# The last 64 tokens of two heads as one pair of 64-column tiles, x in nine blocks, and a new order

## The chip, the cores and the metric

The kernel runs on one core of a Trainium2 chip. The metric is the device time of the whole program in microseconds; lower is better. The core has five engines with queues of their own: TensorE (PE in the profile; its weight loads are PEld), VectorE (DVE), ScalarE (ACT), GpSimd (POOL) and SyncE (SP), which only issues transfers. Engines wait for one another through semaphores.

## The reference, cut to what matters

```python
def _attn_ref(q, k, v, w_phi):              # q, k, v: 8 x 8 heads x 576 tokens x 64; w_phi: 64 x 128
    def phi(x):
        proj = einsum('bhsd,df->bhsf', x, w_phi)
        proj = proj - max(abs(proj), axis=-1, keepdims=True)
        return concatenate([exp(proj), exp(-proj)], axis=-1)
    q_p, k_p = phi(q), phi(k)
    kv = einsum('bhsf,bhsd->bhfd', k_p, v)
    z = sum(k_p, axis=2)
    num = einsum('bhsf,bhfd->bhsd', q_p, kv)
    den = einsum('bhsf,bhf->bhs', q_p, z)[..., None] + 1e-06
    return num / den

# x: the heads of a token side by side, 4608 x 512; w1, w2, w3: 512 x 768; w_out: 768 x 512
h = maximum(maximum(x @ w1, x @ w2), x @ w3)
out = h @ w_out
```

## The kernel before

**Units and pairs.** The attention is cut into 16 units of four heads. The four heads are two pairs (`pr`), and in a pair two heads (`ab`) lie on the two halves of the partitions. A head has 576 tokens: 512 "main" tokens and a tail of 64. In the feature matrices `Eq` (one for each sign, `g`) the main tokens of a head fill four tiles of 128 columns, and the two tails of a pair lie side by side in one tile.

**One unit.** Loads of q, k and v; G, the projections of q and k for row sums of maxima and for `Ek` (`psq`, `psk`, L520: two matmuls side by side, each on 64 of the 128 rows of TensorE's array, form 64\*128); the maxima on VectorE (L539) and `Ek` on ScalarE (L533); the maxima of q carried into a row of `qkT` by a small DMA (`qkT<-mT`); M, the projection of q again (`psm`, L599) and `Eq` (L612); K, the accumulation of keys and values (`kvps`, L628, again pairs of 64\*128 matmuls, 72 to a unit); N, the numerators and the denominator of one head (`psn`, L646); x, a reciprocal and a product on VectorE (L652, L653); and X, which turns `x_sb` into `xT` by a transposing DMA (L676), for the first two units by TensorE (L666). The first four units turn q and k on TensorE (T, `tps`, L482), with matmuls on 64 of the 128 columns of the array (form 128\*64).

**N before.** There are four N in a unit, one for each head, with ten matmuls each: five tiles of 128 tokens times two signs. The fifth tile is the tail. Its left operand is 128 columns wide and begins at the tail of the head, so that half of its rows are of no use. x divides all five tiles, and a unit's `x_sb` has ten blocks of 128.

**The feed-forward part.** Chunk b takes 512 main tokens of both units of batch b, and a ninth chunk takes all tails, gathered by GpSimd into `x_last` (L816). A chunk is 12 groups of four matmuls (`ups`, L699) against w2-w1 and w3-w1, the maximum on VectorE and ScalarE into `hT`, and four or more groups of "straight" (`ops`, L726, x times the product of w1 and w_out) and "down" (`ops`, L731) with an eviction (L739) and a store (L746). The product of w1 and w_out stands in `xT` of the last batch until chunk 5 has read it, and is copied by GpSimd to `w_bf[0]` for the later chunks (L804).

**The order.** Nothing is scheduled at run time. `PLAN` is a table of words such as `1076G@2.9`: node number, engine letter (T is TensorE), numbers of the buffers that it takes, planned start. The program is written out in the order of the table, which gives each engine's order. `fill` puts matmuls without use (`idler`, L828) in TensorE's planned gaps early in the program.

Of the kernel before, what the change touches and what calls it, by code (L numbers as in the profile page):

```python
# [17 lines left out]
DM = H * D  # L18
DFF = 768
P = 128  # L20
# [19 lines left out]
EW = UT * P + D  # L40
XW = SM + P
# [55 lines left out]
0G@0.7 4A@0.7 6S0@0.7 10S0@1.1 2D7@1.1 86G1@1.2 3D@1.5 8S@1.5 13S@2.0 85G@2.0 361S1@2.4 15S0@2.8 1076G@2.9 159G0@3.6 7D2@3.7  # L97
5D@4.2 1G@4.5 158G@5.0 12D@5.1 1079G@5.8 16T5@5.8 17D2@6.5 27T015110@7.3 22T04@7.5 29A@7.8 30D@7.8 28A@8.3 14D@8.6 9A@8.8
26D@9.1 20T5@9.6 31D@9.7 18T6@9.7 24A@9.8 21D@10.3 228G2@10.5 19D@10.5 42T12@10.6 44A@11.0 32T56@11.3 11G@11.3 46D@11.4
1077G@11.4 33A@11.7 35D@11.7 43A@12.2 45D@12.3 23A@12.5 87D3@12.7 25D@12.8 37T31@12.8 88S@12.9 47A1@12.9 93T5@13.0 38A@13.3  # L100
40D@13.4 39A@13.9 94D0@13.9 58T41@14.1 50A0@14.3 41D@14.4 34A@14.5 89T3@14.6 59A@15.0 36D@15.1 55T2@15.2 90D@15.7 61T0@15.8
51A@15.8 60A@16.0 91T3@16.4 63A@16.5 48G@16.9 49D@16.9 67T4@16.9 56A@17.0 64T1@17.3 62A@17.5 68A@17.9 364G1@18.0 115T110601@18.1
69A@18.3 119D@18.5 54A@18.6 66A@18.7 118D@18.8 92D@19.1 53G@19.1 1086T0@19.3 65A@19.3 95T35@19.9 1087A1@20.0 105T71@20.1
52G@20.3 108D@20.6 116A@20.9 109D@21.2 117A@21.3 100T70@21.3 227G@21.4 102A@21.8 103D@21.8 1078G@22.2 57A@22.3 98D@22.4
110T76@22.5 97A@22.8 113D@23.0 162T2@23.1 106A@23.2 101A@23.7 137T30@23.8 163D2@23.8 96A@24.2 166T7@24.2 114D@24.4 164T4@24.5
139A@24.7 1090T2@25.0 167D@25.0 124A1@25.2 165D@25.3 138A@25.4 1088T7@25.5 126G1@25.6 1091A@25.9 70T043@26.0 1089D@26.2
125G@26.7 111A@26.8 140T2@27.2 107A@27.3 104D@27.4 1096T7@27.8 127G@27.8 141A@27.8 72D@28.0 142A@28.2 99D@28.3 112A@28.4
71D@28.9 173T003010@29.1 1097A@29.3 183T56@29.4 73T10@29.6 176D@29.7 174A@29.8 75T4@30.0 187D@30.2 120A@30.3 1094T3@30.4
175A@30.5 121G@30.7 186D@30.8 184A@31.0 160D0@31.4 177D@31.5 185A@31.6 161S@31.7 134T7@31.7 122G@31.8 74D1@32.1 362S1@32.1
79T5@32.2 135A@32.4 128T2@32.5 426S0@32.6 76D0@32.8 1095A@32.9 131T1@33.0 129A@33.4 77T0@33.5 297S0@33.5 80D0@33.5 178T43@33.8  # L110
136A@33.9 1082G@34.0 1098T6@34.1 229D1@34.2 181D@34.3 133A@34.4 182D@34.9 132A@34.9 123A@35.4 168T74@35.5 78D0@35.5 130A@35.6
143T015@35.8 170A@36.1 1080G@36.1 1099D@36.2 180A@36.5 172D@36.8 188T60@36.9 144A@37.2 192D@37.4 145A@37.4 231T2@37.6 191D@37.7
190A@37.8 1092T1@38.1 196A1@38.1 169A@38.3 232D0@38.3 198G0@38.4 189A@38.8 171D@38.9 148T51@39.5 1093A@39.7 152T4@39.8
149D1@40.0 83T0@40.1 199A@40.2 179A@40.4 146T6@40.4 197G@40.5 153D0@40.6 235T2@40.7 84A@40.8 150T1@40.9 236D@41.3 81T5@41.4
147D0@41.5 233T3@41.7 82A@41.9 151D1@42.1 193T6@42.3 154T2@42.4 365G@42.6 194A1@42.7 234D@42.7 242T104701@42.7 155A@43.0
237T10@43.1 195S@43.1 156T6@43.3 245D@43.3 238A@43.6 215T135@43.7 1081G@43.7 296S1@43.8 157D@43.9 243A@44.1 366S1@44.2 241D@44.4
252T24@44.9 246D@45.0 1104T6@45.1 217A@45.1 216A@45.4 255D@45.6 239A@45.7 1112T3@46.1 253A@46.2 240D@46.2 1105A0@46.6 1083D@46.8
247T10@46.9 254A@47.1 257T62@47.3 1110T5@47.4 250D@47.5 1085G@47.8 260D@48.1 203T11@48.4 251D@48.4 1102T6@48.6 1111A@48.6
230S@48.7 256D@49.0 249A@49.1 557S1@49.1 1116T5@49.4 1103A@49.7 1084D@49.9 363S2@50.1 244A@50.2 1114T6@50.3 1117D@50.6 248A@50.7
429G2@50.8 204A@51.1 261D@51.2 209T7@51.2 1124T4@51.4 1113D@51.5 259A@51.6 265A1@51.9 299G0@52.0 258A@52.1 1115D@52.1 262T0@52.3  # L120
1122T5@52.3 205A@52.4 263D0@52.7 210A@52.8 1125D@52.9 264S@53.1 300G@53.1 212T1@53.2 1108T6@53.3 211A@53.4 1123D@53.5 214A@53.9
200T2@54.2 213A@54.3 266G0@54.3 427S0@54.3 367T013010@54.4 1109D@54.4 201A@54.6 387T57@54.7 621S0@54.8 382T14@54.8 371D@55.0
1120T6@55.2 202A@55.2 556S1@55.2 391D@55.6 384A@55.7 385D@55.9 1106T2@56.0 388A@56.2 267G@56.4 383A@56.4 390D@56.5 1121D@56.9
1118T1@56.9 389A@56.9 369A@57.2 370D@57.5 1107A@57.6 377T56@57.8 206T7@58.1 386D@58.1 368A@58.1 1130T2@58.4 208A@58.6 301S2@58.6
380D@58.7 430G@59.1 379A@59.1 224T31@59.3 1119D@59.3 218T0@59.6 207A@59.6 281T50@59.9 225D1@59.9 269T4@60.0 268G@60.2 1131T@60.2
282A@60.2 1101G@60.5 271A@60.5 219D0@60.5 283A@61.0 381D@61.1 270A@61.2 372T57@61.5 624G1@61.7 1132A0@61.8 284T010@61.8
375D@62.1 298S0@62.3 374A@62.4 278T3@62.9 373A@62.9 286D@63.2 220T2@63.2 378A@63.4 376D@63.5 392T4@63.5 1126T0@63.7 279A@63.9
393D1@64.1 221D0@64.3 395A1@64.4 394S@64.5 272T7@64.5 285A@64.6 275T5@64.7 222T4@65.0 273A@65.0 428S3@65.2 287T60@65.3 276A@65.5
223D0@65.5 560G0@65.6 1127T@65.6 431S0@65.6 280A@65.9 288D0@66.3 274A@66.4 559G@66.7 307T104301@66.9 277A@66.9 302T17@67.2
1128A1@67.4 289T2@67.4 310D@67.5 396G0@67.8 291T5@67.8 304A@68.0 305D@68.0 1134T4@68.2 308A@68.5 292D1@68.6 303A@68.9  # L130
408T61@69.1 311D@69.3 1135T@69.3 226S@69.5 410A@69.5 290D0@69.9 397G@69.9 309A@70.0 409A@70.5 306D@70.5 293T5@70.6 322T13@70.9
1136A2@71.0 317T06@71.1 294D1@71.2 312T27@71.4 324A@71.6 1138T4@71.7 315D@71.8 318A@71.8 295S@71.9 398A@72.3 320D@72.4 313A@72.5
402T5@72.6 1139T@72.8 323A@72.9 325D@73.0 319A@73.2 492S0@73.3 316D@73.4 404A@73.7 491S0@73.7 326D@74.0 411T0@74.1 314A@74.2
414T021@74.2 1140D3@74.4 403A@74.6 321D@75.0 413A@75.1 405T5@75.4 412A@75.5 415D@75.7 416A@75.7 399T4@75.7 442T017010@76.0
330A0@76.0 561S1@76.2 400A@76.2 447T61@76.3 333G1@76.4 1152T3@76.5 446D@76.5 332G@76.7 401A@76.8 445D@77.1 449A@77.3 1150T2@77.5
1153D0@77.7 444A@77.8 407A@78.3 432T47@78.3 450D@78.3 1144T3@78.7 1151A@78.7 331G@78.8 435D@78.9 448A@79.2 436D@79.5 327T6@79.6
1148T4@79.7 443A@79.7 1129S@79.9 328D0@80.1 406A@80.2 451D@80.3 1162T2@80.5 1145A@80.7 329S@81.1 1149A@81.1 452T10@81.4
349T163@81.6 434A@81.6 1163D@81.7 493S2@81.8 433A@82.2 688S1@82.2 455D@82.3 456D@82.6 622S1@82.7 437T54@82.7 350A@83.0
494G0@83.2 582T101201@83.2 441D@83.2 453A@83.2 1146T7@83.3 454A@83.6 585D@83.8 1137S@83.9 438A@83.9 440D@84.1 421T60@84.3
495G@84.3 460A0@84.4 1164T1@84.6 439A@84.6 422D0@84.8 1147A@85.1 1141S@85.1 461G1@85.4 337T00@85.4 586D@85.4 351A@85.6  # L140
417T5@85.6 1165D@85.8 584A@85.9 457T6@86.0 334T7@86.0 339A@86.1 1156T4@86.2 418D0@86.4 336A@86.6 458D1@87.0 583A@87.1 340T1@87.1
419T5@87.3 1157D@87.3 335A@87.4 459S@87.4 423T6@87.6 338A@87.8 1158T3@87.9 420D0@88.0 1133S@88.1 342A@88.3 424D1@88.6 346T4@88.8
341A@88.9 343T0@88.9 1160T2@89.1 1159D@89.2 345A@89.4 496S2@89.4 625G@89.7 347A@89.9 1142T7@90.0 344A@90.1 1161D@90.2 348A@90.6
462G@90.8 567T56@90.8 1143D@91.1 572T31@91.2 577T04@91.4 569A@91.4 1154T2@91.6 575D@91.7 574A@91.9 570D@92.3 578A@92.4
# [137 lines left out]
def kernel(  # L282
# [94 lines left out]
    xT = const.tile([P, B, CT, XW], BF16, name="xT")  # L377


    line_w = [xT[:, B - 1, :, 0:DM], w_bf[0][:, :, 0:DM]]  # L380
    x_last = [w_bf[0][:, :, DM:DFF], const.tile([P, CT, DFF - DM], BF16, name="x_last")]

    def zeros():
# [476 lines left out]
```

## Time and profile before

| what | us |
|---|---|
| median of three runs | 288.84 (288.76 to 289.62) |
| the profiled execution, first to last instruction | 287.6 |
| PE busy | 275.5 (96%) |
| DVE, ACT, POOL busy | 205.7, 198.6, 117.1 |
| first matmul of chunk 0, of chunk 7 | 45.5, 245.9 |

The profiled execution is read by its own span of 287.6 us. The median of the runs is 1.24 us above it; launch and end, which have no instruction of the program, are taken to be that difference. A busy time of PE counts a matmul from its start to a modelled end, and matmuls overlap, so the distance from one start to the next is the better measure of what a matmul costs.

### The profile page before, as it was taken

To read this page: it belongs to the slowest core of one execution; us is meant where nothing else is said; L and a number is where in the kernel's file an instruction comes from. 1 tells how busy PE (TensorE), PEld (TensorE's weight loads), DVE (VectorE), ACT (ScalarE), POOL (GpSimd) and SP (SyncE) were. 2 spreads that over 40 slices of the span, in tenths; PEclk is the share of its full clock that TensorE was granted. 3 is DMA by queue.
4 is the path that set the end of the run, shared out by engine and by line. 5 is a ranking of instruction groups with operands and counts; after the bars stand their busy time and mean duration, and the time that the engine had idled before them with its cause. 6 is when DMAs were issued, how large, how long until landed. Compare 5 with 4: busy or idle time off the path is not lost.

```text
span 287.6 us, 8596 instructions
## 1 busy us (share of the span) xinstructions
PE 275.5 (96%) x3550; PEld 154.7 (54%) x3590; DVE 205.7 (71%) x434; ACT 198.6 (69%) x460; POOL 117.1 (41%) x100
## 2 busy tenths in 40 slices
PE   8889999999989899999999999999999999999995
PEld 3366675466555455655555466565544654444443
DVE  4679899988979788887879778987863551516511
ACT  1599998999998789895798979997756631040010
POOL 8264688868454349706365434050083000000000
PEclk9999999999999999999999999999999999999999
DMA  7999977999999998999899769787510019410054
GB/s 181 277 248 209 228 298 121 330 282 235 237 176 336 210 260 182 265 267 253 198 238 211 207 122 203 235 171 132 119 41 0 2 41 199 115 34 0 0 153 141
DMA packets 68337, 51.45 MB, mean 179 GB/s; under 512 B 48778, under 2 KB 53066, under 8 KB 68298
## 3 DMA queue, kind: packets, MB, share of 16 engines
q1 hardware_dynamic: 63903, 45.62, 65.6%
q0 software_dynamic: 4000, 4.92, 9.9%
q8 instruction: 28, 0.46, 0.7%
q10 hardware_dynamic: 395, 0.37, 0.4%
q14 instruction: 11, 0.09, 0.1%
HBM read 34.64 MB, written 9.44 MB: 153 GB/s over the span
## 4 chain that ended last, share of the span: by engine, by line
PE 87%; DMA 5%; DVE 3%; ACT 2%; issue 1%; SPq 0%; ACTq 0%; DVEq 0%
PE ups L699 31%; PE ops L731 16%; PE ops L726 10%; PE psn L646 7%; PE kvps L628 6%; PE psq L520 6%; PE psm L599 5%; DMA k_raw<-in_k_dram 3%; DMA qkT<-mT 2%; PE pm L797 2%; DVE mk L539 1%; PE tps L482 1%; DVE mqp L539 1%; ACT Ek L533 1%; ACT Eq L612 1%
## 5 line engine op out<-in xcount | busy, mean ns | idle before, releaser
L699 PE MATMUL ups<-xT,w_bf 128*128 128x512 bf16 x417 | 100.6, 379 | 0.8
L533 ACT ACTIVATE Ek<-psk 128x512 bf16<-128x512 f32 (+1 forms) x160 | 82.0, 572 | 15.3 <-PE psk L520 11.9
L574 POOL TENSOR_TENSOR vab<-v_raw,em 128x1152 bf16<-128x1152 f32 (+1 forms) x35 | 66.8, 1926 | 56.0 <-ACT em L570 45.9
L612 ACT ACTIVATE Eq<-psm 128x512 bf16<-128x512 f32 (+1 forms) x160 | 80.1, 577 | 10.4 <-PE psm L599 9.8
L699 PEld LDWEIGHTS <-w_bf 128*128 128x128 bf16 x432 | 40.2, 98 | 44.4
L539 DVE TENSOR_REDUCE mqp<-psq 128x4 bf16<-128x512 f32 (+1 forms) x80 | 48.5, 633 | 6.4 <-PE psk L520 4.7
L539 DVE TENSOR_REDUCE mk<-psk 128x4 f32<-128x512 f32 (+1 forms) x80 | 49.1, 630 | 5.0 <-PE psk L520 3.3
L731 PE MATMUL ops<-wout_bf,hT 128*128 128x512 bf16 (+2 forms) x219 | 49.8, 367 | 0.6 <-issue 0.3
L705 DVE TENSOR_TENSOR hT<-hT,ups 128x512 bf16<-128x512 bf16 x54 | 35.5, 681 | 16.8 <-PE ups L699 16.3
L739 ACT COPY osb<-ops 128x512 f32<-128x512 f32 (+2 forms) x18 | 10.0, 563 | 36.5 <-PE ops L731 28.9
L707 ACT ACTIVATE hT<-ups 128x512 bf16<-128x512 f32 x38 | 22.4, 612 | 15.5 <-PE ups L699 14.0
L731 PEld LDWEIGHTS <-hT 128*128 128x128 bf16 x228 | 21.1, 98 | 22.2
L653 DVE TENSOR_TENSOR x_sb<-psn,rden 128x320 bf16<-128x320 f32 x64 | 31.5, 492 | 2.2
L646 PEld LDWEIGHTS <-Eq 128*128 128x128 bf16 x640 | 25.9, 98 | 9.7
L739 DVE COPY osb<-ops 128x512 f32<-128x512 f32 (+1 forms) x20 | 13.4, 668 | 21.8 <-PE ops L731 21.6
L646 PE MATMUL psn<-kv_sb,Eq 128*128 128x65 bf16 x640 | 28.2, 194 | 0.0
L520 PE MATMUL psq<-w,qkT 64*128 64x128 bf16 x288 | 24.6, 217 | 2.2 <-DVE mk L539 0.8
L520 PEld LDWEIGHTS <-qkT 64*128 64x128 bf16 x576 | 16.8, 94 | 15.9 <-issue 11.9
L520 PE MATMUL psk<-w,qkT 64*128 64x128 bf16 x288 | 24.5, 217 | 0.2 <-DVE v_raw L460 0.2
L726 PE MATMUL ops<-xT 128*128 128x512 bf16 x85 | 23.1, 379 | 0.9 <-issue 0.5
L599 PE MATMUL psm<-qkT,wphi_m 128*128 128x512 bf16 (+1 forms) x70 | 22.1, 358 | 1.3 <-DMA qkT<-mT 1.2
L652 DVE RECIPROCAL rden<-psn 128x5 f32<-128x5 f32 x64 | 12.1, 189 | 11.8 <-PE psn L646 11.2
(74 smaller groups left out, 237.2 us busy)
## 6 DMA issues: line engine op xcount, KB each, us to landing
v_raw<-in_v_dram SPq DMA_DIRECT2D x16, 576.0 KB
out_dram<-osb SPq DMA_DIRECT2D x65, 128.0 KB
q_raw<-in_q_dram SPq DMA_DIRECT2D x12, 576.0 KB
k_raw<-in_k_dram SPq DMA_DIRECT2D x12, 576.0 KB
w_bf<-in_moe_w_dram POOLq DMA_DIRECT2D x3, 768.0 KB, 15.5
qk_bf<-in_k_dram POOLq DMA_DIRECT2D x3, 288.0 KB, 16.5
qk_bf<-in_q_dram POOLq DMA_DIRECT2D x3, 288.0 KB, 11.6
wout_bf<-in_moe_w_out_dram POOLq DMA_DIRECT2D x1, 768.0 KB, 20.7
```

The lines of the kernel that those rows point to most:

```text
L520: nc.tensor.matmul(ps()[:, i, :], lhsT=cols[r, :], rhs=w2[r, c, :], start=True, stop=True)
L533: nc.scalar.activation(Ek[s]()[:, tiles_of(t0, n), :], of(1), EXP, scale=1.0 - 2.0 * s)
L539: nc.vector.tensor_reduce((mq, mk)[c]()[:, tiles_of(t0, n)], of(c), AXX, ALU.max, apply_absolute_value=True)
L574: (nc.vector if n_.eng == "DVE" else nc.gpsimd).tensor_tensor(vab()[:, g, t0:t1, 0:D], vb()[:, t0:t1, :], em()[:, g, t0:t1].unsqueeze(2).t ...
L599: nc.tensor.matmul(psm()[:, 0:w], lhsT=wphi_m, rhs=rhs, start=True, stop=True)
L612: nc.scalar.activation(Eqb()[s][:, cols], psm()[:, 0:w], EXP, scale=1.0 - 2.0 * s)
L646: nc.tensor.matmul(psn()[:, c, :], lhsT=Eqb()[g][:, t0:t0 + P], rhs=kv()[:, pr, ab, g, :], start=(g == 0), stop=(g == 1))
L653: nc.vector.tensor_tensor(x_sb()[:, pr, :, ab, :], psn()[:, :, 0:D], rden().to_broadcast([P, 5, D]), ALU.mult)
L699: nc.tensor.matmul(ups(), lhsT=w_bf[i + 1][:, ct, j * P:(j + 1) * P], rhs=tokens_of(ct), start=(ct == 0), stop=(ct == CT - 1))
L705: nc.vector.tensor_tensor(hT()[:, j, :], hT()[:, j, :], ups(), ALU.max)
L726: nc.tensor.matmul(ops_()[:, 0:width], lhsT=tile_of(ct, tt), rhs=line_w[c_i > MOVE][:, ct, cols], start=(ct == 0), stop=False)
L731: nc.tensor.matmul(ops_()[:, 0:width], lhsT=hT()[:, j, tt * P:(tt + 1) * P], rhs=wout_bf[:, j, cols], start=False, stop=(j == JT - 1))
```

## The change

The two tails of a pair become the two 64-column halves of one tile. The N of one head in each pair (`ab == pr`) computes the tails of both heads, with matmuls of 64 columns: head a writes the partitions from 64a on. Its x divides five tiles, that of the other head four. `x_sb` and `xT` of a unit have nine blocks in place of ten, block 4 being both pairs' tails; tails have rows and columns of another arrangement, so GpSimd gathers them with four copies a batch, into a tile of its own, which the ninth chunk reads for `ups` as well. `Eq` loses its 64 spare columns. The copy of the product of w1 and w_out is made in four instructions in place of two. The table `PLAN` is new throughout: engines, order, buffers and planned starts.

```diff
-EW = UT * P + D
-XW = SM + P
+EW = UT * P
+XT = 2 * (SM // P) + 1
+XTAIL = SM // P
...
-1476A2@281.5 1473S@281.6 1477A@281.9
+1475T@267.92 1468A2@268.08 1470T1@268.25 1469A@268.45 1471T@268.47 1476D1@268.50 1477S@268.92 1472A3@269.05 1473A@269.30
...
-    xT = const.tile([P, B, CT, XW], BF16, name="xT")
+    xT = const.tile([P, B, 2, XT, P], BF16, name="xT")
+    x_last = const.tile([P, CT, B * ST], BF16, name="x_last")
...
-        x_sb = buf("x_sb", 2, [P, 2, 5, 2, D], BF16)
+        x_sb = buf("x_sb", 2, [P, XT, P], BF16)
...
         for pr in range(2):
             for ab in range(2):
+                tail = ab == pr
                 psn = bank("psn", [P, 5, W])
-                def nmm(pr=pr, ab=ab, psn=psn):
-                    for c in range(5):
-                        t0 = (8 * pr + 4 * ab + c if c < 4 else MT + pr) * P + (D if c == 4 and ab else 0)
+                first, n_x = (0 if pr == 0 else 1 if tail else 0), 5 if tail else 4
+                def nmm(pr=pr, ab=ab, psn=psn, first=first, tail=tail):
+                    for c in range(4):
+                        t0 = (8 * pr + 4 * ab + c) * P
                         for g in range(2):
-                            nc.tensor.matmul(psn()[:, c, :], lhsT=Eqb()[g][:, t0:t0 + P],
+                            nc.tensor.matmul(psn()[:, first + c, :], lhsT=Eqb()[g][:, t0:t0 + P],
                                              rhs=kv()[:, pr, ab, g, :], start=(g == 0), stop=(g == 1))
+                    if tail:
+                        for g in range(2):
+                            for a in range(2):
+                                t0 = (MT + pr) * P + a * D
+                                nc.tensor.matmul(psn()[a * D:(a + 1) * D, 4 * (1 - pr), :], lhsT=Eqb()[g][:, t0:t0 + D],
+                                                 rhs=kv()[:, pr, a, g, :], start=(g == 0), stop=(g == 1))
...
-                a = nd("N", {"PE": 0.32}, nmm, [n_kvs[ab]] + eqs[first_eq:first_eq + 2] + eqs[8:], [Eqb, kv, psn, x_sb])
+                need = n_kvs + eqs[first_eq:first_eq + 2] + eqs[8:] if tail else [n_kvs[ab]] + eqs[first_eq:first_eq + 2]
+                a = nd("N", {"PE": 0.30 if tail else 0.24}, nmm, need, [Eqb, kv, psn, x_sb])
...
-                nc.sync.dma_start_transpose(
-                    out=xT[:, b, ct0:ct0 + 2, :].rearrange("p q (t c) -> p (q t) c", c=P),
-                    in_=x_sb().rearrange("p q t a d -> p (q t a d)"))
+                nc.sync.dma_start_transpose(out=xT[:, b, u % 2, :, :], in_=x_sb().rearrange("p t c -> p (t c)"))
...
+    def tails(b):
+        for pr in range(2):
+            for ab in range(2):
+                nc.gpsimd.tensor_copy(x_last[ab * D:(ab + 1) * D, pr::2, b * ST:(b + 1) * ST],
+                                      xT[pr * D:(pr + 1) * D, b, :, XTAIL, ab * ST:(ab + 1) * ST])
...
-    chunk(B, lasts, lambda ct: xT[:, :, ct, SM:SM + ST],
-          lambda ct, tt: x_last[tt // 2][:, ct, tt % 2 * P:(tt % 2 + 1) * P],
+    chunk(B, lasts, lambda ct: x_last[:, ct, :], lambda ct, tt: x_last[:, ct, tt * P:(tt + 1) * P],
```

The order shows the change at two places. The first is TensorE in an N of the middle of the program. Before, the last matmuls of such an N are these (`Eq` with its two signs, all 128 columns), and a projection for M of a later unit follows:

```order
L646 MATMUL psn<-kv_sb,Eq_1_77 128x65
L646 LDWEIGHTS Eq_1_78
L646 MATMUL psn<-kv_sb,Eq_1_78 128x65
L599 LDWEIGHTS wphi_m
L599 MATMUL psm<-qkT,wphi_m 128x256
```

Now the N of a head that carries the tails ends in four matmuls of 64 columns, after its eight of 128 columns, and here a G of two tiles follows:

```order
L667 MATMUL psn<-kv_sb,Eq_0_76 128x65
L674 LDWEIGHTS Eq_0_75
L674 MATMUL psn<-kv_sb,Eq_0_75 64x65
L674 LDWEIGHTS Eq_0_75
L674 MATMUL psn<-kv_sb,Eq_0_75 64x65
L674 LDWEIGHTS Eq_0_76
L674 MATMUL psn<-kv_sb,Eq_0_76 64x65
L674 LDWEIGHTS Eq_0_76
L674 MATMUL psn<-kv_sb,Eq_0_76 64x65
L539 LDWEIGHTS qkT
L539 MATMUL psq<-w_73,qkT 128x128
```

There are 32 such endings, two in each unit. In them the array is used in halves of its columns, while the rows ahead use all of it.

The second place is TensorE where the ninth K of the program begins, which is that of unit 7. Before, a G (halves of the rows) stands directly ahead of it, and another directly behind:

```order
L520 MATMUL psq<-w_73,qkT 128x128
L520 LDWEIGHTS qkT
L520 MATMUL psk<-w_73,qkT 128x128
L628 LDWEIGHTS Ek_2561
L628 MATMUL kvps<-vab,Ek_2561 128x65
```

Now `ups` of chunk 2, on the whole array, stand directly ahead of it, and others directly behind:

```order
L727 LDWEIGHTS w_bf
L727 MATMUL ups<-xT,w_bf 128x512
L647 LDWEIGHTS Ek_2528
L647 MATMUL kvps<-vab,Ek_2528 128x65
L647 LDWEIGHTS Ek_2528
```

So G and K, which stood next to one another, stand apart. Counted along TensorE's whole order, the form of the array (128\*128, 64\*128 or 128\*64) differs between a matmul and the next 106 times before and 240 times now: 46 and 54 times ahead of the first `ups` of chunk 0, 60 and 186 times between that and the first `ups` of chunk 7, and never after it. The `idler` matmuls become 24 from 36.

More of the change, by code (lines that the diff above doesn't have):

```diff
@@ L388, in zeros @@
             nc.vector.memset(mqp[i], 0.0)
-            for g in range(2):
-                nc.vector.memset(Eq[i][g][:, UT * P:EW], 1.0)
     def phi_weights():
@@ L417, in attention @@
         un = units[u]
-        b, ct0 = u // 2, (u % 2) * 2
+        b = u // 2
         early, by_pe = u < 2, u < BY_PE
@@ new lines, in attention, with div @@
+                rden = buf("rden", 2, [P, 5, 1], FP32)
+                def div(pr=pr, ab=ab, psn=psn, rden=rden, tail=tail, n_x=n_x):
+                    b0 = pr * (XTAIL + 1) - (1 if pr and tail else 0)
+                    nc.vector.reciprocal(rden()[:, 0:n_x, :], psn()[:, 0:n_x, D:W])
+                    nc.vector.tensor_tensor(x_sb()[:, b0:b0 + n_x, ab * D:(ab + 1) * D], psn()[:, 0:n_x, 0:D],
+                                            rden()[:, 0:n_x, :].to_broadcast([P, n_x, D]), ALU.mult)
@@ L655, in attention @@
                 first_eq = 4 * pr + 2 * ab
-                a = nd("N", {"PE": 0.32}, nmm, [n_kvs[ab]] + eqs[first_eq:first_eq + 2] + eqs[8:], [Eqb, kv, psn, x_sb])
-                divs[pr].append(nd("x", {"DVE": 0.62}, div, [a], [psn, x_sb, rden], locks=[psn]))
+                need = n_kvs + eqs[first_eq:first_eq + 2] + eqs[8:] if tail else [n_kvs[ab]] + eqs[first_eq:first_eq + 2]
+                a = nd("N", {"PE": 0.30 if tail else 0.24}, nmm, need, [Eqb, kv, psn, x_sb])
+                divs[pr].append(nd("x", {"DVE": 0.62 if tail else 0.56}, div, [a], [psn, x_sb, rden], locks=[psn]))
```

331 lines of the change are left out of this document (172 added, 159 removed).

## The prediction

> **What bounds the kernel now.** I read the page first, then the stages, then single matmuls.
>
> The page, its engines and its chain of waits:
>
> ```profile
> span 287.6 us, 8596 instructions
> PE 275.5 (96%) x3550; PEld 154.7 (54%) x3590; DVE 205.7 (71%) x434; ACT 198.6 (69%) x460; POOL 117.1 (41%) x100
> PE 87%; DMA 5%; DVE 3%; ACT 2%; issue 1%; SPq 0%; ACTq 0%; DVEq 0%
> ```
>
> TensorE is busy for 96% of the span and carries 87% of the chain; no other engine is over 71%. I cut the span into three stages: up to the first `ups` of chunk 0, from there to the first `ups` of chunk 7, and the rest. The columns are stage, its length, busy time of each engine (instructions), granted clock, DMA share and GB/s; above them are the timeline's rows that give the cuts and the last matmuls.
>
> ```profile
> 45.47 1.90 PE L699 MATMUL ups<-xT,w_bf 128*128 128x512 bf16 x7
> ...
> 245.88 4.48 PE L699 MATMUL ups<-xT,w_bf 128*128 128x512 bf16 x20
> ...
> 0.00:45.50 45.50, 41.40 (x753) 26.11 (x757) 35.63 (x86) 34.12 (x80) 28.60 (x33) 1.00 0.98 228
> 45.50:245.90 200.40, 196.06 (x2608) 110.28 (x2641) 153.67 (x323) 159.50 (x371) 88.53 (x68) 1.00 0.82 190
> 245.90:287.60 41.70, 38.02 (x194) 18.29 (x195) 16.35 (x26) 4.96 (x10) 0.00 (x0) 1.00 0.27 73
> 281.46 2.63 PE ops L731 x24
> ```
>
> In the middle stage PE lacks 4.3 us of 200.4. In the last it lacks 3.7, all of it the last eviction and store behind the last matmul (281.46 + 2.63 = 284.1). The clock is granted in full everywhere. So from 45.5 us on, what TensorE has to do is what the time is, and a part of the change counts there only as far as it alters PE's own work or makes PE wait.
>
> **A change of the array's form has a price.** This is the row that I rest on. Before, the form changes 106 times, so the trace shows its price. First a round trip to half columns (L482, 128\*64) out of and back to the whole array, then one to half rows (L520, 64\*128), in the timeline of PE: start, duration, operation, count.
>
> ```profile
> 15.46 0.39 PE L604 MATMUL psm<-minus,mqp 128*128 128x64 bf16 x8
> 15.79 0.64 PE L482 MATMUL tps<-ident,qk_bf 128*64 128x128 bf16 x16
> 16.36 0.39 PE L601 MATMUL psm<-qkT,w 128*128 128x512 bf16 x1
> ...
> 90.04 1.89 PE L699 MATMUL ups<-xT,w_bf 128*128 128x512 bf16 x8
> 91.86 0.23 PE L520 MATMUL psq<-w,qkT 64*128 64x128 bf16 x1
> ...
> 92.43 0.22 PE L520 MATMUL psk<-w,qkT 64*128 64x128 bf16 x1
> ...
> 92.49 0.22 PE L520 MATMUL psk<-w,qkT 64*128 64x128 bf16 x1
> 92.64 1.04 PE L699 MATMUL ups<-xT,w_bf 128*128 128x512 bf16 x4
> ```
>
> For the paces inside one form, three pieces of the chain (start, length, what, count):
>
> ```profile
> 49.05 2.59 PE ups L699 x12
> 62.28 1.09 PE kvps L628 x72
> 230.88 0.94 PE psn L646 x30
> ```
>
> A 512-column matmul takes 2.59/12 = 0.216 us, one of `psn` 0.94/30 = 0.031, and one of K's 1.09/72 = 0.015, since two go side by side. Now the trips. Eight `ups` from 90.04 should end at 91.77; G starts at 91.86, 0.09 late. G's twelve pairs start between 91.86 and 92.49, one every 0.057 us, so `ups` could start at 92.55 and starts at 92.64, 0.09 late again. Eight narrow matmuls from 15.46, at 0.031, end at 15.71; the half-column ones start at 15.79, 0.08 late. Their eight pairs at 0.057 end at 16.25, and the next starts at 16.36, 0.11 late. So I take 0.095 us for each change of form, in either kind and either direction, none of it hidden: it is time between two starts of the engine that bounds.
>
> By the Trainium skill, "TensorEngine Tiling (Array Packing)", Key Properties, changing the tiling mode drains TensorE, and tiles within one mode run independently. The trace agrees on both: 0.08 to 0.11 us lost at each change, and 0.015 us for a K matmul beside 0.031 for one of the same width on the whole array.
>
> **The change, part by part.**
>
> *Tails, on PE.* Two N of a pair had 20 matmuls, 20 x 0.031 = 0.62 us. Now they have 16 wide ones and 4 half ones, two pairs in two slots: 18 x 0.031 = 0.56. That saves 0.06 for each of 32 pairs, 2.0 us in all, 1.7 of it in the middle stage (28 pairs). No row has 64-column matmuls this short. If a pair paces like the L520 pairs (0.06 in place of 0.031), the saving is gone. I take the first, since K's equally short halves do reach it.
>
> *Changes of form.* The order has 134 more: 59 are the tails' (64, less five where a G or K follows at once, which would have had its own), the others are G and K groups that stand apart now. By stage: 46 to 54 at the start, 60 to 186 in the middle, none at the end. Middle: 126 x 0.095 = 12.0 us, all on the path, as PE lacks only 4.3 us there.
>
> *Work that crosses the first cut.* Adding up PE's matmuls along both orders at the paces above, 25.0 us of them stand ahead of chunk 0 before and 23.5 now; 0.4 of the difference is saved there (four pairs of N, two transposes less), and 1.1 moves into the middle. Middle stage: 12.0 - 1.7 + 1.1 = **+11.4 us**.
>
> *The start.* Its rows:
>
> ```profile
> 1.04 4.84 PE L828 MATMUL idler<-idle 128*128 128x512 bf16 x11 [1.04 <-DVE idle L402]
> ...
> 2.11 7.72 DMA k_raw<-in_k_dram
> ```
>
> Before, the 45.5 us are 25.0 of matmuls, 46 x 0.095 = 4.4 of changes, 36 idlers (4.8 for the first 11, 25 x 0.216 = 5.4 for the rest) and 5.9 in which PE has nothing (1.04 of it ahead of its first). Now they are 23.5, 54 x 0.095 = 5.1, 24 idlers (4.8 + 13 x 0.216 = 2.8) and an unknown wait. With no wait but the first 1.04 the stage is 37.2 us; if the other engines and the loads hold it as before, 45.5. The loads of k of unit 0, which everything begins with, took 7.72 us with the loads of unit 1 and the first weights issued beside them; in the new order GpSimd waits for k before it issues those. That speaks for some gain, ACT's and DVE's unchanged load (34.1 and 35.6 us busy of 45.5) against all of it. I take the middle, 41.4: **-4.1 us**, between -8.3 and 0.
>
> *Waits in the middle.* One row of the transfers of the maxima shows how PE comes to wait, in the chain and at the matmul that follows:
>
> ```profile
> 88.91 6.78 DMA qkT<-mT
> 95.74 0.60 PE L599 MATMUL psm<-qkT,wphi_m 128*128 128x512 bf16 x2 [1.20 <-DMA qkT<-mT]
> ```
>
> This small transfer took 6.8 us behind big loads on the same engines, and PE, in program order, stood still for M with `ups`, `psn` and G queued behind it. The new order puts M close behind its transfer in several units, but PE needs 6% longer for what stands between. I keep 4.3 us of waits, **0**, with -4.3 (PE is late everywhere) and +5 (three or four more such stops of 1.2 to 2 us) as bounds.
>
> *Off the path.* Three groups of the page's kind (count | busy us, mean ns of one | idle before), then a row of the timeline and two of the chain:
>
> ```profile
> L653 DVE TENSOR_TENSOR x_sb<-psn,rden 128x320 bf16<-128x320 f32 x64 | 31.5, 492 | 2.2
> L816 POOL COPY x_last<-xT 128x256 bf16<-128x256 bf16 x4 | 1.6, 397 | 35.3 <-DMA xT<-x_sb 35.3
> L441 POOL COPY gated<-k_raw 1x1 f32<-1x1 f32 x1 | 0.2, 177 | 0.0
> 243.33 0.40 POOL L816 COPY x_last<-xT 128x256 bf16<-128x256 bf16 x1 [24.88 <-DMA xT<-x_sb]
> 237.96 0.31 PE psn L646 x10
> 255.80 10.96 PE ups L699 x50
> ```
>
> Half of the 64 divisions shrink by a fifth, up to 32 x 0.1 = 3.1 us of DVE, which waits for PE anyway: nothing. The tails' copies become 32 of 0.18 to 0.40 us where 8 of 0.40 were; GpSimd is 41% busy. The last four, 0.7 to 1.6 us, start where the one of 243.33 stood, and must be done by chunk 8's `ups`, which run in the stretch that begins at 255.80 (chunk 7 has the first 48): covered. They, and the product's copy in four parts, stand behind waits of GpSimd's queue with nothing urgent behind them. The transposing transfers lose a tenth of their blocks: nothing, as PE does not wait for them. At the second cut, 26 matmuls of `ops` (5.6 us) stand between the last N and chunk 7. Before, it was 5.1 us from the end of the last N (237.96 + 0.31) to the landing that GpSimd waited for (243.33): covered with 0.5 to spare; if a store is ahead on SP, up to 1.5 us (in the +5). The first N of a unit now waits for both copies of kv, with other work of PE between K and it: nothing. The other N no longer wait for the last `Eq`: nothing.
>
> *Sum.* -4.1 + 11.4 + 0 + 0 at the end = +7.3 us: a span of 294.9, and 288.84 + 7.3 = **296.1 us**, the 1.24 us between span and median being kept.
>
> **The rivals.** Each is the same sum with another term; 0.3% (0.9 us) is about what a measurement of this kernel can tell from no change.
>
> *Forecast, 60%.* PE pays every change, the start gains half: 296.1.
>
> *The start gains nothing, 17%.* ACT and DVE bound it; their busy shares there (75 and 78%) speak neither way. 288.84 + 11.4 = 300.2.
>
> *M waits for its row, 13%.* The 88.91 row is for it, that PE is slower against it. With +5: 301.1.
>
> *All the favourable ends together, 4%.* No waits at all and a start of 37.2: 288.84 + 11.4 - 8.3 - 4.3 = 287.6 at the extreme, the most of the case within 0.9 us of no change.
>
> *Faster: the halves cost no change of form, 6%.* The new pairs would be taken in stride, as a half-array matmul may load its weights while the whole array still runs, or the gap would fall into waits. Middle: -1.7 + 1.1 = -0.6; start: -4.1 - 8 x 0.095 = -4.9; 288.84 - 5.5 = 283.3. It decides where a new change of form costs less than (5.5 - 0.9)/134 = 0.034 us. Against it: four places above show 0.08 to 0.11. The Trainium skill's "TensorEngine Tiling (Array Packing)", Theoretical Speedup, has a factor of up to 2 for a left operand of 64 columns or less, and by that alone, without the drain, the change would come out so; K's 0.015 beside 0.031 agrees on the factor, the four places speak against leaving out the drain.
>
> **How the numbers follow.** Faster 0.06, same 0.03, slower 0.91. The range reaches from the forecast with waits gone (296.1 - 4.3 = 291.8), and a bit of the favourable start, 291.0, to the case of M's waits with a little of the start's, 302.0; left out are the two cases below 291 (10%) and the far ends of the others.
>
> **What would show it.** Right: PE busy near 98% in the middle stage, that stage 210 to 214 us long, a gap of 0.09 at both ends of each tail group, first `ups` at 39 to 43 us, DVE and ACT with more idle time. Wrong: gaps under 0.03 us (faster case); a first `ups` at 45 (start); PE waits on `qkT<-mT` adding up to over 5 us, or on `xT` at the second cut.

## The result and the profile after

| | before | changed | ratio (95% interval) |
|---|---|---|---|
| median, us | 289.23 (288.76 to 289.70, 4 runs) | 296.82 (296.75 to 297.06, 4 runs) | 1.0258 (1.0235 to 1.028) |
| span of the profiled execution, us | 287.6 | 294.9 | |

The change makes the kernel 2.6% slower. The forecast was 296.1 with a span of 294.9.

The page of the changed kernel, in the rows that were read of before:

```profile
span 294.9 us, 8579 instructions
PE 285.2 (97%) x3534; PEld 154.5 (52%) x3576; DVE 212.0 (72%) x446; ACT 195.8 (66%) x443; POOL 123.0 (42%) x128
PE 91%; DMA 2%; DVE 2%; issue 2%; POOL 1%; ACT 1%; SPq 0%
```

PE carries 91% of the chain where it carried 87%. The three stages, cut at the same matmuls as before (first `ups` of chunk 0 and of chunk 7), in the same columns:

```profile
0.00:42.20 42.20, 38.29 (x663) 24.29 (x666) 33.22 (x78) 32.40 (x73) 25.17 (x32) 1.00 1.00 222
42.20:253.60 211.40, 208.93 (x2682) 111.84 (x2718) 163.82 (x346) 156.28 (x358) 97.73 (x96) 1.00 0.74 181
253.60:294.90 41.30, 37.98 (x193) 18.34 (x195) 15.00 (x23) 7.14 (x13) 0.14 (x1) 1.00 0.33 81
```

The start is 3.3 us shorter (45.5), the middle 11.0 longer (200.4), the end 0.4 shorter (41.7). PE now lacks 2.5 us of the middle, where it lacked 4.3: it does not wait more (it is busy for 98.8%, where near 98 was forecast), it is slower at the work. Here is an N with its tails in the timeline of PE (start, duration, operation, count), with a G behind it:

```profile
111.84 0.41 PE L667 MATMUL psn<-kv_sb,Eq 128*128 128x65 bf16 x8
112.18 0.25 PE L674 MATMUL psn<-kv_sb,Eq 128*64 128x65 bf16 x4
112.36 0.23 PE L539 MATMUL psq<-w,qkT 64*128 64x128 bf16 x1
...
112.43 0.22 PE L539 MATMUL psk<-w,qkT 64*128 64x128 bf16 x1
112.58 1.90 PE L727 MATMUL ups<-xT,w_bf 128*128 128x512 bf16 x8
```

Eight wide matmuls at 0.031 should hand over at 112.09; the halves start at 112.18. Four halves then take PE until 112.36, 0.18 us. Before, an N of ten went from 237.79 to 238.11, 0.32 us; this one, which makes the tail of the other head too, takes 0.52, and the N without tails 0.25. In the records of single matmuls all 32 groups look alike: 0.125 us from the last wide start to the first half (0.031 is the pace inside a form), then the two of a pair 0.003 apart and the next pair 0.052 behind the first, and 0.130 from the last half to the next matmul of another form (27 times of the whole array, five times of G or K; in two groups the record of a 512-column matmul is missing there). So the way in costs 0.094 and the way out 0.099. Around G and K it is 0.096 in and 0.093 out.

The weight loads of the same stretch show how a change differs from a step inside a form:

```profile
111.84 0.28 PEld L667 LDWEIGHTS <-Eq 128*128 128x128 bf16 x7
112.18 0.14 PEld L674 LDWEIGHTS <-Eq 128*64 128x64 bf16 x4
112.36 0.11 PEld L539 LDWEIGHTS <-qkT 64*128 64x128 bf16 x4
112.58 0.11 PEld L727 LDWEIGHTS <-w_bf 128*128 128x128 bf16 x2
```

At the three changes the first load starts with its matmul (112.18, 112.36, 112.58). Inside a form it starts about one matmul earlier: 0.028 us ahead of its own for 65 columns and 0.214 for 512, in the median of tails_alone (below), whose trace has every record; at that kernel's changes it is 0.002 to 0.004. So nothing is loaded ahead across a change. What the load waits for there, no row shows.

### The profile page after: what moved, and what is told of

Its sections match the earlier page's. It is cut to its first block, busy times and chain, and to the rows that moved or that the text cites. A ratio compares the mean times of both kernels' runs of the same rounds, so it can differ in the third digit from the quotient of the medians.

```text
span 294.9 us, 8579 instructions
## 1 busy us (share of the span) xinstructions
PE 285.2 (97%) x3534; PEld 154.5 (52%) x3576; DVE 212.0 (72%) x446; ACT 195.8 (66%) x443; POOL 123.0 (42%) x128
## 4 chain that ended last, share of the span: by engine, by line
PE 91%; DMA 2%; DVE 2%; issue 2%; POOL 1%; ACT 1%; SPq 0%
PE ups L727 32%; PE ops L759 16%; PE ops L754 11%; PE psq L539 7%; PE kvps L647 6%; PE psn L667 6%; PE psm L618 5%; PE psn L674 2%; DMA q_raw<-in_q_dram 2%; PE tps L501 1%; POOL vab L593 1%; PE pm L825 1%; DVE mqp L558 1%; PE idler L862 1%; PE psm L620 1%
## 5 line engine op out<-in xcount | busy, mean ns | idle before, releaser
L727 PE MATMUL ups<-xT,w_bf 128*128 128x512 bf16 x364 | 91.8, 380 | 1.1
L735 ACT ACTIVATE hT<-ups 128x512 bf16<-128x512 f32 x29 | 17.4, 605 | 21.7 <-PE ups L727 19.8
L681 DVE TENSOR_TENSOR x_sb<-psn,rden 128x320 bf16<-128x320 f32 (+1 forms) x64 | 29.3, 458 | 2.2
L539 PE MATMUL psq<-w,qkT 64*128 64x128 bf16 x288 | 28.4, 219 | 0.2
L539 PE MATMUL psk<-w,qkT 64*128 64x128 bf16 x288 | 28.1, 218 | 0.0
L767 ACT COPY osb<-ops 128x512 f32<-128x512 f32 (+2 forms) x22 | 12.5, 573 | 23.1 <-PE ops L759 19.1
L667 PEld LDWEIGHTS <-Eq 128*128 128x128 bf16 x512 | 22.0, 98 | 9.0
L667 PE MATMUL psn<-kv_sb,Eq 128*128 128x65 bf16 x512 | 25.8, 194 | 0.0
L767 DVE COPY osb<-ops 128x512 f32<-128x512 f32 (+1 forms) x16 | 10.6, 660 | 17.3 <-PE ops L759 12.5
L737 DVE TENSOR_SCALAR hT<-ups 128x512 bf16<-128x512 f32 x25 | 16.9, 683 | 6.8 <-PE ups L727 6.3
```

The lines of the kernel that those rows point to most:

```text
L539: nc.tensor.matmul(ps()[:, i, :], lhsT=cols[r, :], rhs=w2[r, c, :], start=True, stop=True)
L667: nc.tensor.matmul(psn()[:, first + c, :], lhsT=Eqb()[g][:, t0:t0 + P], rhs=kv()[:, pr, ab, g, :], start=(g == 0), stop=(g == 1))
L681: nc.vector.tensor_tensor(x_sb()[:, b0:b0 + n_x, ab * D:(ab + 1) * D], psn()[:, 0:n_x, 0:D], rden()[:, 0:n_x, :].to_broadcast([P, n_x, D]) ...
L727: nc.tensor.matmul(ups(), lhsT=w_bf[i + 1][:, ct, j * P:(j + 1) * P], rhs=tokens_of(ct), start=(ct == 0), stop=(ct == CT - 1))
```

## The sum again, with every matmul counted

All kernels below do nearly the same matmuls in the middle stage, so I split its length in three: the matmuls of the written order at the paces of the prediction (0.216 us for 512 columns, 0.108 for 256, 0.054 for 128, 0.030 for 65, half of that in halves of the array), the changes of form at 0.095, and what is left. Of what is left, two parts can be read from the traces: PE's waits for another engine or a transfer (its rows of waits, 0.15 us and longer), and the first steps, which are explained below the table.

| kernel | first `ups` of chunk 0, of chunk 7 | middle | matmuls | changes | left | of it waits | of it first steps |
|---|---|---|---|---|---|---|---|
| before | 45.5, 245.9 | 200.4 | 190.2 | 60: 5.7 | 4.5 | 2.0 | 0.6 |
| changed | 42.2, 253.6 | 211.4 | 189.7 | 186: 17.7 | 4.0 | 0.0 | 2.2 |
| tails_alone | 45.8, 249.6 | 203.8 | 188.5 | 114: 10.8 | 4.4 | 0.7 | 1.5 |
| order_alone | 42.1, 250.5 | 208.4 | 191.4 | 134: 12.7 | 4.3 | 0.9 | 1.4 |
| whole_tails | 42.6, 251.4 | 208.8 | 191.1 | 134: 12.7 | 5.0 | 0.7 | 1.4 |
| two_trips | 42.3, 261.6 | 219.2 | 189.7 | 242: 23.0 | 6.5 | 0.0 | 3.2 |

The first step behind a change, from the first start (or pair) in the new form to the next, is longer than the steps that follow. For 512 columns it is 0.226 us in place of 0.216, for G's pairs 0.066 in place of 0.056, for the pairs of T, which use half the columns, 0.080 in place of 0.056. Where no change stands ahead, the first step has the usual length. With its first step a change costs about 0.11 us: (17.7 + 2.2)/186 in the changed kernel, (5.7 + 0.6)/60 before. What is left is so alike in five kernels because two parts move against each other: where changes are added, PE waits less and has more long first steps.

## Experiments

Each was timed beside the kernel before on the same chip; the ratio is to that. The kernel before had medians of 289.18 to 290.03 us there, so the ratios compare better than the times.

**The tails alone.** The changed code with the order of before:

```diff
...
-1475T@267.92 1468A2@268.08 1470T1@268.25 1469A@268.45 1471T@268.47 1476D1@268.50 1477S@268.92 1472A3@269.05 1473A@269.30
+1476A2@281.5 1473S@281.6 1477A@281.9
```

> The changed code (tails as halves of the columns, nine blocks) under the table PLAN of the kernel before: 166 changes of form, 60 more than before. Theory (each change of form costs 0.095 us of TensorE, and TensorE bounds): a tail group took 0.28 us in the changed kernel's trace where the two fifth tiles of a pair took 4 x 0.031 = 0.12, so 32 x 0.16 less 4 x 0.095 for groups that share a change = +4.7: 293.9 us, first ups at 45 to 46 us. Rival (the new order costs the time, the tails do not): 289 us or less.

Measured: 293.12 us, ratio 1.0118 (1.0051 to 1.0184). The 54 added changes of the middle stage make it 3.4 us longer, less the matmuls saved (5.1 - 1.7). Against the kernel before beside it (289.78) the whole is +3.3 where +4.7 was expected; the waits that went (2.0 to 0.7) are about that difference. Its middle stage:

```profile
45.80:249.60 203.80, 202.96 (x2644) 112.11 (x2641) 151.53 (x323) 159.74 (x371) 95.04 (x94) 1.00 0.79 184
```

**The order alone.** The code of before with the new table (seven N stand slightly later in it, with other banks, since that code needs their data):

```diff
...
-1476A2@281.5 1473S@281.6 1477A@281.9
+1466T3@266.62 1464A0@266.87 1467T@267.06 1465A@267.48 1474T4@267.71 1475T@267.92 1468A2@268.08 1470T1@268.25 1469A@268.45 1471T@268.47 1476D1@268.50 1477S@268.92
+1472A3@269.05 1473A@269.30
```

> The code of before (tails as a fifth tile of each head, ten blocks) under the new table PLAN; seven N stand a few instructions later, since each of them needs the tail's Eq there. 181 changes of form, 75 more than before. Theory: 75 x 0.095 = +7.1, the start -3.3, waits of the middle stage -1.8: +2.0, 291.2 us, first ups at 42 to 43 us. Rival (the tails alone cost the time, G and K standing apart cost nothing): 289.2 - 3.3 - 1.8 = 284 us.

Measured: 293.58 us, ratio 1.0132 (1.0081 to 1.0182). That is +3.8 against the kernel before beside it (289.78), where +2.0 was expected. Two terms were wrong: the matmuls that the new order moves out of the start (+1.2 in the middle) were not put back, and the waits fell by 1.1, not 1.8, while the first steps of the added changes took 0.8. That a denser order would pay for its changes is refuted. The tails (+3.4 us in the middle) and the order (+8.0 there, -3.4 at the start) together give the +11.0 and -3.3 of the whole change to within 0.5 us.

**Tails without halves.** The two tails of a pair as two matmuls of the whole array and 130 columns, with x in three products:

```diff
-                            for a in range(2):
-                                t0 = (MT + pr) * P + a * D
-                                nc.tensor.matmul(psn()[a * D:(a + 1) * D, 4 * (1 - pr), :], lhsT=Eqb()[g][:, t0:t0 + D],
-                                                 rhs=kv()[:, pr, a, g, :], start=(g == 0), stop=(g == 1))
+                            nc.tensor.matmul(psn()[:, 4:6, :], lhsT=Eqb()[g][:, t0:t0 + P],
+                                             rhs=kv()[:, pr, :, g, :], start=(g == 0), stop=(g == 1))
```

> The changed kernel and its table, but the tails of a pair as two matmuls of the whole array: all 128 columns of the pair's tile against both heads' kv side by side (130 columns wide), of which half of each half is used; x then divides main tiles and each tail by three products in place of one. 181 changes of form, 59 fewer than the changed kernel. Theory: a tail group of 0.28 us becomes 2 x 0.056 = 0.11: 32 x 0.17 = -5.4 us, 291.4 us. Rival (the halves are not what costs; the order and its waits are): 296.8 us, or more with the two added products on VectorE.

Measured: 294.51 us, ratio 1.0157 (1.0108 to 1.0206): 2.3 us better than the changed kernel (2.9 by the ratios) where 5.4 were expected. The same N and G as above, in its timeline:

```profile
111.86 0.41 PE L667 MATMUL psn<-kv_sb,Eq 128*128 128x65 bf16 x8
112.11 0.28 PE L673 MATMUL psn<-kv_sb,Eq 128*128 128x130 bf16 x2
112.32 0.23 PE L539 MATMUL psq<-w,qkT 64*128 64x128 bf16 x1
```

No gap ahead of the tails now (112.11 is 8 x 0.031 behind 111.86), and the change that is left belongs to G. The 52 changes fewer take 5.0 us off the middle stage and their first steps 0.8, and the wider matmuls put 1.4 on it: 4.4 in all, where 28 x 0.17 = 4.8 was expected. The start is 0.4 later. PE waits in the middle stage again, where the changed kernel has no such row:

```profile
PE ups L730 <- DVE x_sb L680: 0.3, 1, 0.3
PE kvps L647 <- POOL vab L593: 0.2, 1, 0.2
PE ops L757 <- DVE x_sb L680: 0.2, 1, 0.2
```

Two of the three are for VectorE's products, 4 to a pair where there were 2. But order_alone, which has no such products, has two waits for `x_sb` as well (0.3 each), so that the added products are the reason is not shown, and 1.1 us of what is left over stays open.

**Twice as many trips.** The tail of each head is made in its own trip, in the middle and at the end of the wide ones, so that one half of the array stands empty:

```diff
-                    if tail:
-                        for g in range(2):
-                            for a in range(2):
+                        if tail and c % 2:
+                            a = c // 2
+                            for g in range(2):
```

> The changed kernel with the same half-column matmuls, but head 0's two stand after the second wide tile and head 1's two at the end: 304 changes of form, 64 more, and no two halves side by side. Theory: a second trip of 0.19 us and two slots of 0.03 more, 32 x 0.25 = +8.0 us: 304.8 us. Rival (the price is one of the tails' data, their weight loads or the waits around them, not of each change of form): under 299 us.

Measured: 305.43 us, ratio 1.0532 (1.048 to 1.0584), as expected. One N in its timeline:

```profile
114.22 0.29 PE L667 MATMUL psn<-kv_sb,Eq 128*128 128x65 bf16 x4
114.44 0.25 PE L673 MATMUL psn<-kv_sb,Eq 128*64 128x65 bf16 x2
114.62 0.30 PE L667 MATMUL psn<-kv_sb,Eq 128*128 128x65 bf16 x4
114.85 0.25 PE L673 MATMUL psn<-kv_sb,Eq 128*64 128x65 bf16 x2
115.03 0.23 PE L539 MATMUL psq<-w,qkT 64*128 64x128 bf16 x1
```

Two halves one behind the other cost 0.18 us (114.44 to 114.62), as much as two pairs side by side do. The trip is the price, and hardly what is done in it. (The split above counts these halves as if they went side by side, 112 x 0.015 = 1.7 us too little; with the first steps, 3.2, that is most of the 6.5 left over.)

**The loads of unit 0 first.** The kernel before with GpSimd's loads of units 1 and 2 and the first weights behind the wait for unit 0's k, as the new order has them, and SyncE's load of q of unit 5 behind v of unit 0. Its words in the table for GpSimd:

```diff
-86G1@1.2 85G@2.0 1076G@2.9 159G0@3.6 1G@4.5 158G@5.0 1079G@5.8 228G2@10.5 11G@11.3
+1G@1.25 11G@4.76 86G1@4.80 85G@4.81 1076G@4.82 159G0@4.83 158G@4.84 1079G@4.85 228G2@10.50
```

> The kernel before with one thing of the new order: GpSimd issues the loads of units 1 and 2 and the first weights only when a part of unit 0's k has landed, and SP issues a q of unit 5 behind v of unit 0. 106 changes of form, as before. Theory (the new start is earlier because unit 0's loads run alone): the last of them lands at 7.7 us in place of 9.8, first ups at 43 to 44 us, 287 to 288 us. Rival (the start is earlier because of the order on ScalarE and VectorE behind the loads): first ups at 45 to 46 us, 289 us.

Measured: 289.05 us, ratio 1.0003 (0.9961 to 1.0045). The start gains 0.6 us, not 1.5 to 2.5: VectorE can turn to the second part of unit 0's k at 7.9 us in place of 9.9, but then PE waits for a load of unit 1. First a row of its chain of waits, then the largest of PE's waits behind the first idlers:

```profile
6.07 7.56 DMA qk_bf<-in_q_dram
```

```profile
PE tps L470 <- DMA qk_bf<-in_q_dram: 1.0, 1, 1.0
```

**The loads all at once.** The converse, in the changed kernel:

```diff
-1G@1.25 11G@4.79 86G1@4.94 85G@5.79 1076G@6.64 158G2@7.44 159G@8.29 1079G@9.14
+86G1@0.70 85G@0.70 1076G@0.70 1G@1.25 158G2@1.25 159G@1.25 1079G@1.25 11G@4.79
```

> The changed kernel with the reverse: GpSimd issues the loads of units 1 and 2 and two weights at once, as before. 240 changes of form. Theory (loads): first ups at 44 to 45 us where the changed kernel has 42.2, 298.5 to 299 us. Rival (order behind the loads): first ups at 42 to 43 us, 297 us.

Measured: 299.63 us, ratio 1.0329 (1.0273 to 1.0384); first `ups` at 45.7. The load that the chain of waits begins with, first in the changed kernel, then in this one, and this one's largest wait of PE:

```profile
2.12 5.63 DMA q_raw<-in_q_dram
```

```profile
2.11 7.77 DMA q_raw<-in_q_dram
```

```profile
PE tps L477 <- ACT qk_bf L439: 2.7, 1, 2.7
```

Its engines in four stretches around that wait (PE's busy time is the second figure, the granted clock the third from the end):

```profile
8.00:12.00 4.00, 1.30 (x26) 0.81 (x26) 1.59 (x4) 2.09 (x5) 0.07 (x1) 1.00 1.13 263
12.00:14.00 2.00, 2.00 (x22) 0.88 (x20) 1.61 (x4) 1.94 (x6) 1.35 (x2) 0.65 1.15 211
14.00:16.00 2.00, 2.00 (x6) 0.67 (x5) 2.00 (x5) 1.32 (x3) 0.00 (x0) 0.50 1.19 205
16.00:18.00 2.00, 2.00 (x47) 1.57 (x47) 1.64 (x3) 1.59 (x5) 0.81 (x1) 1.00 1.22 207
```

The load lands 2.1 us later, PE stands for 2.7 us, and right behind that its granted clock falls to a half for over three microseconds. So the 3.5 us are both: the load, and the clock that the wait costs. Without its order of loads the new start gains nothing; by loads_first, that order alone isn't enough either.

**Only the start of the new order.** The code of before; the first 402 words of the new table (63 us planned), then the rest of before's:

```diff
...
+49G@14.79 100T12@15.19 51A@15.19 59A@15.44 104D@15.67 1077G@15.91 60A@15.92
...
+289T4@63.03 621S0@63.03 1101G@63.03 624G1@63.03 298S0@63.03
 428S3@65.20 287T6@65.30 288D0@66.30 307T30@66.90
...
```

> The code of before; its table is the new order up to 402 entries (planned start 63 us, as in order_alone) and from there the order of before for what is left. 119 changes of form. Theory (price per change, start earlier by the new order): the middle stage has 13 changes more than before at most, +1.2, the start -3.3: 286.5 to 288 us, faster than both kernels. Rival (the new order's loss is not in G and K standing apart but in its start's sequel, as loads that come too early or late): 290 us or more.

Measured: 293.54 us, ratio 1.0121 (1.0066 to 1.0176); first `ups` at 42.35. `fill` saw a gap in the planned times where the two orders meet and put 18 idlers there, 3.9 us: a fault of the experiment. So I took those out:

```diff
-        while gap > (0.35 if t < WARM else 0.5) and t < n.start - 0.2:
+        while gap > (0.35 if t < WARM else 0.5) and t < min(n.start - 0.2, 45.0):
```

> The kernel before with the new order for its first 402 entries, as in new_start, but with no idler planned later than 45 us: 18 matmuls without use fewer, 119 changes of form as there. Theory (PE's path is a plain sum, and the idlers were all on it): 18 x 0.216 = 3.9 us less than new_start, 289.6, first ups of chunk 0 at 42.3 as there, chunk 7 near 245.9, its middle stage near 203.5. So the start that the new order gains is given back by what that order puts behind it, and this kernel is no faster than the one before. Rival: the idlers only filled waits that come back as idle time of PE, 292 to 293.5. Second rival: the start that is gained stays gained once the idlers are gone, 286 to 287.

Measured: 292.88 us, ratio 1.0135 (1.0056 to 1.0213). In the profiled executions chunk 7 begins 1.3 us sooner (248.4 for 249.8), not 3.9, and by the ratios nothing is gained. The timeline of PE at the seam, and then its engines in three stretches there:

```profile
71.74 0.21 PE L508 MATMUL psq<-w,qkT 64*128 64x128 bf16 x1 [0.39 <-ACT Ek L521]
...
73.41 0.21 PE L508 MATMUL psq<-w,qkT 64*128 64x128 bf16 x1 [1.38 <-ACT Ek L521]
```

```profile
70.95:74.35 3.40, 1.29 (x14) 0.69 (x15) 2.34 (x6) 2.82 (x7) 0.52 (x2) 0.99 1.03 321
74.35:77.80 3.45, 3.20 (x14) 1.36 (x15) 2.55 (x5) 2.51 (x7) 1.04 (x1) 0.51 1.11 327
77.80:81.20 3.40, 3.40 (x97) 2.14 (x96) 1.85 (x4) 2.73 (x9) 0.34 (x2) 1.00 1.04 259
```

Some idlers had covered true waits for ScalarE; without them PE is busy for 1.29 of 3.4 us, and then it works for 3.4 us at half the clock. My theory and the second rival fell. The time is the first rival's, though not only by waits that came back: the clock is part of it.

**A shorter start of the new order.** As new_start, with 72 words instead of 402:

> The same with only the first 72 entries of the new order (planned start 14.7 us). 103 changes of form. Theory: first ups at 43 to 44 us, no more changes than before, 287 us. Rival (the early part has to go on in its own order to bring anything): first ups at 45 us or later, 289 us or more.

Measured: 289.43 us, ratio 0.9986 (0.995 to 1.0022). First `ups` at 44.4: 1.1 of the 3.3 us, no difference that can be measured. In its chain stand 13 of its 36 idlers, close together where the orders meet, so the last two runs leave idlers out, there and in the kernel before (15 and 6 fewer, all those planned later than 14 us):

```diff
-        while gap > (0.35 if t < WARM else 0.5) and t < n.start - 0.2:
+        while gap > (0.35 if t < WARM else 0.5) and t < min(n.start - 0.2, 14.0):
```

> new_start_short with no idler planned later than 14 us: 21 idlers in place of 36, the computation untouched. In new_start_short 13 idlers stand on the chain of waits at the seam of the two orders (16.35 to 19.8, 3.0 us). Theory (those 13 fill no wait, they are time, and the start gain of the new order is real but eaten by them): first ups of chunk 0 at 41.6 to 42.3, all behind it as before, 286.6 to 287.3, faster than the kernel before by 0.7 to 0.9%. Rival (ScalarE and VectorE hold the start; the idlers stand where PE would wait anyway): first ups near 44, 289. Second rival (TensorE stands idle long enough there that its granted clock falls to a half, as in new_start_no_idlers): 289.5 to 291.

> The kernel before with no idler planned later than 14 us: 30 idlers in place of 36, nothing else changed. The six that go stand between 19.4 and 24.3 us. Theory (they fill waits for the maxima of unit 1 on VectorE, 0.4 to 0.7 us each in the rows of waits): first ups at 45.2 to 45.5, within 0.3% of the kernel before, 289. Rival (they are time on PE's path): 6 x 0.216 = 1.3 us less, 287.9.

Measured: short_fewer_idlers 289.99 us, ratio 0.9994 (0.9959 to 1.0028), first `ups` at 46.8; before_fewer_idlers 293.25 us, ratio 1.0122 (1.0093 to 1.0151), first `ups` at 46.7. PE of the first in two stretches, then of the second:

```profile
20.00:24.00 4.00, 2.87 (x35) 1.94 (x35) 3.77 (x7) 2.82 (x6) 0.53 (x1) 0.50 1.18 251
24.00:28.00 4.00, 4.00 (x76) 3.63 (x78) 2.28 (x5) 3.08 (x7) 2.46 (x3) 0.50 1.21 209
```

```profile
20.00:24.00 4.00, 2.43 (x56) 1.83 (x54) 3.25 (x7) 3.51 (x8) 2.38 (x3) 1.00 1.23 207
24.00:28.00 4.00, 4.00 (x70) 3.46 (x69) 2.42 (x6) 3.48 (x9) 2.05 (x2) 0.57 1.20 210
```

Six matmuls without use, 1.3 us of PE, are what keeps the clock whole in the kernel before: without them it is granted 0.57 from 24 to 28 us, and chunk 0 begins 1.2 us later. All six executions without them have a mean granted clock of 0.982 to 0.994; beside them 15 of 17 of the kernel before have 0.998 or more. The traced execution is the fastest of the six (290.76), so this trace shows 1.2 us and not the whole 3.2 us between the medians. Neither of my theories for the two runs held. In the first run the clock fell as its second rival says; its time alone (289.99, with the kernel before at 290.03 beside it) wouldn't tell that rival from the first. None of these versions is measurably faster than the kernel before.

## Why the prediction was right

*PE bounds, and a change of form has a price of 0.095 us: right, but a little low.* The gap is 0.094 and 0.099 at the tails, 0.096 and 0.093 at G and K. The longer first step behind it was overlooked; with it the price is about 0.11, over 60 to 242 changes. For the middle stage that is 1.6 us more than the forecast's 12.0. The Trainium skill's "TensorEngine Tiling (Array Packing)", Theoretical Speedup, with its factor of up to 2 for a left operand of 64 columns, is outweighed here: the four halves do go in pairs, but the group costs 0.28 us behind the last wide start's slot, in and out of the form, where the same tails took 0.12 as four whole matmuls.

*Tails on PE, -1.7 in the middle: right, by the split.* With 1.7 us of matmuls less, tails_alone has 2.2 us left beside waits and first steps, near the 1.9 of before. The second pair of a group starts 0.052 behind the first, not 0.031, near the other bound that the prediction gave (0.06). A group has only this one step, so its pace can't be read from it; T's longer rows of half-column pairs have the same excess (0.080 for 0.056) in their first step alone. That speaks for a part of the change of form, 28 x 0.02 = 0.6 us, and not for a slower pace.

*The middle, +11.4: measured +11.0.* By the split, matmuls -0.5 and changes +12.0 with 0.5 less left over. In that last part two errors of the forecast meet: first steps +1.6 and waits -2.0. That the stage came out within 0.4 us is luck in this.

*The start, -4.1: measured -3.3, inside its bounds.* In the terms of the prediction: 23.5 of matmuls, 5.1 of changes, 7.6 of idlers leave 6.0 us of the 42.2 in which PE has nothing, where before it was 5.9. So PE waits as much as before, and the gain is 1.5 of moved and saved work and 2.6 of idlers, less 0.7 of changes. I had let the wait shrink by 0.7. The forecast was the middle between two bounds, so that it came this near is in part luck. The single tests of the loads and of the first 72 words gave 0.6 and 1.1 us, and taking idlers out of the kernel before or out of that shorter start cost the clock. With 402 words (new_start) chunk 0 begins at 42.35 and the clock is whole up to there, with 13 idlers fewer in the start; so the gain needs more of the new order than its first 72 words. Which part of the rest it needs stays open.

*Waits in the middle, 0: wrong, they went.* PE's two largest waits there in the kernel before, and then the three largest of the changed kernel in its whole span:

```profile
PE psm L599 <- DMA qkT<-mT: 1.2, 1, 1.2
PE psq L520 <- DVE mk L539: 0.8, 1, 0.8
```

```profile
PE idler L862 <- DVE idle L421: 1.0, 1, 1.0
PE tps L501 <- ACT qk_bf L463: 0.9, 1, 0.9
PE pm L825 <- PE psk L539: 0.8, 1, 0.8
```

All three of the changed kernel lie in the start, and `qkT<-mT` isn't among them: the rival in which M waits for its row is refuted. But of the 4.3 us that I read as waiting before, only 1.2 + 0.8 were waits. Another 1.6 are 30 gaps of 0.053 us, each where one record of a 512-column matmul is missing (2 x 0.216 - 0.379 = 0.053): the stage of before has 2608 records of matmuls for 2641 weight loads. In tails_alone, with all records there, PE lacks 0.84 us. So the term was -2.0, as in the bound in which PE is late everywhere, whose -4.3 was more than could have gone.

*Off the path: nothing, right.* The tails' copies, in the rows of their tile: count, durations (lowest, median, highest ns), first and last start. Then the divisions' group of the page:

```profile
L849 POOL COPY x_last<-xT x32: 280/291/293, 63.1 to 253.4; 64x128 bf16<-64x128 bf16 x32
```

```profile
L681 DVE TENSOR_TENSOR x_sb<-psn,rden 128x320 bf16<-128x320 f32 (+1 forms) x64 | 29.3, 458 | 2.2
```

A copy takes 0.29 us, between the bounds of 0.18 and 0.40; the last starts at 253.4, ahead of the second cut, and nothing waits for it. The divisions fell from 31.5 to 29.3 us busy without any use, and VectorE as a whole rose from 205.7 to 212.0, since the new table gives it more of other work; its idle time grew by 1.0 us only, to 82.9.

*From span to time.* The span came out as forecast, 294.9, the errors of start (+0.8), middle (-0.4) and end (-0.4) cancelling, which is luck. The median is 1.9 above it, not 1.24. The profiled executions of the experiments lie 1.7 to 1.9 above their own spans; 1.24 had set the span of one execution against the median of others. That is the 0.7 us by which 296.1 missed.

## What to carry to other kernels

Count the changes of the array's form along the written order before splitting a matmul into halves, and multiply: at about 0.11 us each in this kernel, a trip pays only if it saves more than seven matmuls of 65 columns. A share of busy time includes missing records, so take waits from the rows of waits, not from what busy time leaves over. And filler work in a program's gaps may be holding the clock up: before taking it out, add up how busy TensorE would be without it.

## What the runs showed of the hardware

After a stretch in which TensorE had little to do, its granted clock fell to 0.50. Of the 3.41 us directly ahead of the fall PE was busy for 1.89 in loads_at_once (from 9.18), 1.29 in new_start_no_idlers (from 70.90), 1.84 in before_fewer_idlers (from 20.73) and 2.06 in short_fewer_idlers (from 14.60). In the first three it came back after 3.4 us, in the last after 10.2. The Trainium skill's "TensorE: Matmul & The Clock Gate", Part 1, has such a gate, to a half after an idle window of about 3.4 us and back after a busy one of that length. The traces agree on the half and on the length. They differ on what counts as idle: no single wait was longer than 2.7 us in loads_at_once and 1.4 in new_start_no_idlers, so a window needn't be empty, only thin. But not every thin stretch does it: PE was busy for 1.45 of the 3.41 us from 18.25 in before_fewer_idlers and for 1.93 of those from 6.25 in whole_tails, and the clock stayed whole. What decides between them, no run shows.
